# Constant tables gated on steps of the first attention, and a rewritten order of steps, in a fused attention and Fourier-mix kernel

## The chip, the cores and the metric

The kernel runs on one core of a Trainium2 chip. The time is the device time of one execution in microseconds (us). A core has a matmul engine (PE, with its weight loads, PEld), a vector engine (DVE), a scalar engine (ACT), a general engine (POOL, GpSimd) and a queue engine (SP). POOL and SP also issue DMAs.

## The reference, cut to what matters

The program is block attention with a learned soft permutation of blocks, then a Fourier mix with a two-layer MLP.

```python
# batch 4, heads 8, seq 768, head_dim 64, 8 blocks of 96; d_model 512, hidden 2048
for _ in range(5):                       # Sinkhorn on sort_net, 8x8 per head
    P = exp(P - max(P)); P /= sum(P, -1); P /= sum(P, -2)
k_sorted, v_sorted = P @ k_blocks, P @ v_blocks
attn = softmax(q_block @ k_sorted_block.T / 8);  x = attn @ v_sorted_block
u = x + real(fft(fft(x, axis=seq), axis=d_model))
out = u + relu(layernorm(u) @ w_ch1) @ w_ch2
```

All of the inputs have to come in once: K, Q and V (6.3 MB each) and two weights (4.2 MB each), as float32, cast to float16 on the way. The Fourier transforms are matmuls against constant tables.

## The kernel before

The work is cut into some 530 small steps, each a function named by one letter and digits. A long string fixes the order in which the steps are written.

```python
ORDER = ("B2 B0 k00AA B1 M00 M01 M02 M03 x000 e000 k01DA H M04 M05 Z0 "
         "s03 s00 s04 s05 x011 e011 L20 D b0 x010 s02 s01 v20A V v31A "
         ... )
for tok in ORDER.split():
    fns[tok[0]](*[...digits of tok...])
W = (32, 8, 8)             # PE, DVE, ACT
for e, w in zip((EN.PE, EN.DVE, EN.Activation), W):
    for n in range(w, len(runs[e])):
        dep(runs[e][n], runs[e][n - w])   # n runs after the one w places before it
```

A scheduler may move an instruction within the window W of its engine, but no further. After compiling, each engine runs its list in order. The steps that matter here (the first digit is the batch, A or D names the engine, ACT or DVE, that copies a matmul result out):

- L20, L21, V: POOL issues the loads of K and Q of batch 2 (two halves) and of V of batches 2 and 3.
- k, q: sort and transpose K and Q; x, e: scores and their exponentials; M, Z, s: sum of V and V minus its mean, written into the tile vcx; v, w: sort V, matmuls that read vcx; o: attention output.
- f, c, d, l, n: Fourier folding on DVE, sequence transform, width transform with LayerNorm statistics, LayerNorm factors on POOL, normalisation.
- h, y: the two MLP layers, 896 of the 2,400 matmuls.
- q21, q20, ...: for later batches Q is rearranged by DVE (copy qr<-q) and transposed by DMA:

```python
def t_q(b, hp, eng="S"):
    ...
    if eng == "S":
        qr = wt([128, 6, 2, D], F16, "qr", 1)
        nc.vector.tensor_copy(qr, q16.rearrange("p h r d -> p r h d"))
        nc.sync.dma_start_transpose(qt, qr.rearrange("p r h d -> p (r h d)"))
```

The tables are loaded right after the Sinkhorn iterations (ph is the list of their last DVE steps; gated(x, y) lets x wait for y, start(x) keeps x in program order). The first, dtab, lands in a part of the weight tile w2sb, and POOL copies it to unused columns of vcx.

```python
dst = w2sb.rearrange("p c m -> p (c m)")[:, 0:1024]
gated(nc.sync.dma_start(dst, cn["dtab"]...), ph[7])
start(nc.gpsimd.tensor_copy(vcx[:, 0:8, 96:128, :], dst...))
...  # then tab, cs, lt and small rows on the SP queue
for c in range(4):
    w = nc.gpsimd.dma_start(w1sb[:, c, :], w1v[:, c, :])
    gated(w, ph[9]) if c == 0 else start(w)
for c in range(4):
    start(nc.gpsimd.dma_start(w2sb[:, 4 * c:4 * c + 4, :], ...))
...
def t_v(n, bb, eng):      # sorts V: reads whole rows of vcx, also columns 96:128
    for dd in range(8):
        nc.tensor.matmul(ps[:, dd, :], vcx[:, 2 * n + dd // 4, :, dd % 4], bd)
```

The softmax here doesn't subtract the row's maximum and nothing guards it: scores larger than these inputs give would overflow.

## Time and profile before

| | before |
|---|---|
| time, median | 297.5 us (3 runs); 297.77, 298.32, 298.03 and 298.00 in the later sets |
| span of the profiled run | 296.2 us |
| PE busy | 274.7 us, 93% of the span |
| DVE, ACT, POOL busy | 64%, 41%, 13% |

The table of stretches gives, for each stretch of time, the busy time of PE, PEld, DVE, ACT and POOL with the number of instructions, then the granted PE clock (1.00 is full), the DMA share and GB/s. Lines for short stretches in which PE starves, and two long ones from later:

```profile
20.00:24.00 4.00, 2.57 (x43) 2.23 (x44) 4.00 (x9) 2.18 (x7) 0.05 (x1) 0.91 1.23 246
24.00:28.00 4.00, 3.61 (x62) 3.14 (x57) 3.79 (x12) 3.47 (x8) 1.02 (x2) 0.50 1.32 203
44.00:48.00 4.00, 1.43 (x39) 1.16 (x37) 3.86 (x10) 2.93 (x7) 1.08 (x2) 0.90 1.24 218
48.00:52.00 4.00, 4.00 (x33) 3.24 (x32) 3.50 (x9) 1.98 (x4) 0.75 (x1) 0.50 1.24 211
56.00:60.00 4.00, 1.28 (x19) 0.84 (x17) 1.72 (x4) 0.63 (x2) 0.00 (x0) 1.00 1.10 222
60.00:64.00 4.00, 3.56 (x36) 2.12 (x37) 3.23 (x9) 1.88 (x5) 0.00 (x0) 0.60 1.05 203
...
100.00:120.00 20.00, 20.00 (x189) 12.64 (x189) 12.80 (x29) 11.52 (x26) 0.76 (x2) 1.00 0.08 27
240.00:260.00 20.00, 20.00 (x114) 10.90 (x112) 11.76 (x23) 1.96 (x4) 0.00 (x0) 1.00 0.14 47
```

From about 64 us on PE is nearly always busy (its longest wait is then 0.4 us) and at full clock. Before that it starves three times (at about 22, 45 and 57 us), and each time the clock falls to one half for a while. The Trainium skill's page "TensorE: Matmul & The Clock Gate", Part 1, says that an idle window of about 3.4 us throttles the clock. The trace agrees in the lengths: its clock records show half clock at 23.3-30.1, 47.2-54.0 and 60.8-64.2 us, which is 6.8, 6.8 and 3.4 us. It does not show a whole idle window first: PE's longest waits there were 1.2, 1.6 and 2.7 us, and PE was busy for 2.4, 1.4 and 1.1 us of the 3.4 us before each fall.

The waits of PE in the list of waits (us in total, times, longest):

```profile
PE pf L276 <- DMA q<-in_q_dram: 8.6, 1, 8.6
PE pf L465 <- DVE u L661: 2.7, 1, 2.7
PE pf L626 <- DVE ee L597: 1.6, 1, 1.6
PE pf L448 <- DMA k<-in_k_dram: 1.2, 1, 1.2
```

The third starvation comes from DVE. Its timeline (start, duration, engine, line, operation, what it writes and reads; in brackets the idle time before it and what ended it):

```profile
54.66 0.25 DVE L641 TENSOR_SCALAR yr<-y 128x384 f16<-128x384 f16 x1
58.25 0.36 DVE L269 COPY qr<-q 128x768 f16<-128x768 f16 x1 [3.33 <-DMA q<-in_q_dram]
58.52 0.68 DVE L661 SCALAR_TENSOR_TENSOR u<-r,pf 128x512 f32<-128x512 f16 x1
```

DVE stood 3.33 us before the copy qr<-q, because Q of batch 2 had not landed. The step u behind it, which frees a buffer that PE needs, had its input from PE at about 55.1 us (the matmul L657 ran from 54.69 to 55.07). This stop of DVE before qr is called the gate below. POOL's timeline shows where that load stands in the queue:

```profile
17.32 1.04 POOL L309 COPY vcx<-w2sb 128x1024 f16<-128x1024 f16 x1 [4.10 <-DMA w2sb<-k_dtab]
18.30 1.08 POOL L328 DMA_DIRECT2D w1sb<-in_moe_w_ch_dram  x2
38.90 0.74 POOL L169 DMA_DIRECT2D q<-in_q_dram  x1 [1.45 <-DMA w1sb<-in_moe_w_ch_dram]
```

The issue at 38.90 us landed 19.3 us later, at 58.2. DMA moves about 215 GB/s in nearly every slice from 4 to 64 us, so each load lands when all that stands before it has been moved.

### The profile page before, as it was taken

Reading aid. Unit: us, or ns where it says so; the run is one execution under the profiler, and the core shown is the slowest. Engines: PE = TensorE matmul, PEld = TensorE weight load, DVE = VectorE, ACT = ScalarE, POOL = GpSimd, SP = SyncE. Lnnn points to the kernel's source line nnn. Section 1 sums busy time; section 2 is a strip of 40 time slices with the busy share of each in tenths; the row PEclk is TensorE's granted clock in tenths of the full one; section 3 lists DMA queues with packets and bytes.
Section 4 is the critical chain, followed back from the end, with each engine's and each line's share of the span. In section 5 each row is a group of like instructions: output and inputs, shape, how many; then the busy total and the mean of one; then the engine's idle time right before and its main releaser. Section 6 shows DMA issues by size and latency. Waiting matters only on the chain.

```text
span 296.2 us, 5916 instructions
## 1 busy us (share of the span) xinstructions
PE 274.7 (93%) x2395; PEld 165.9 (56%) x2395; DVE 190.0 (64%) x451; ACT 122.4 (41%) x260; POOL 39.3 (13%) x75
## 2 busy tenths in 40 slices
PE   0897986699999999999999999999999999999994
PEld 0366875456564666755565557546645555555551
DVE  6568699388887765666976578639716736643312
ACT  2358766348867755640477125203610111121210
POOL 8722332012020000400020002000200200020000
PEclk9995996879999999999999999999999999999999
DMA  7999999995179110481323101220031021033002
GB/s 113 219 300 205 214 209 215 214 180 76 22 43 124 39 38 35 53 123 38 110 58 62 55 35 38 54 73 35 19 38 71 37 55 71 35 37 124 1 2 106
DMA packets 32706, 26.48 MB, mean 89 GB/s; under 512 B 17347, under 2 KB 28099, under 8 KB 32676
## 3 DMA queue, kind: packets, MB, share of 16 engines
q0 software_dynamic: 11712, 13.63, 28.3%
q1 hardware_dynamic: 20966, 12.46, 17.1%
q8 instruction: 19, 0.31, 0.4%
q14 instruction: 9, 0.07, 0.1%
HBM read 29.10 MB, written 6.29 MB: 119 GB/s over the span
## 4 chain that ended last, share of the span: by engine, by line
PE 76%; DMA 13%; POOL 5%; DVE 2%; issue 2%; ACT 0%; POOLq 0%
PE pm L724 28%; PE pm L712 28%; DMA w1sb<-in_moe_w_ch_dram 7%; DMA q<-in_q_dram 7%; PE pf L497 4%; PE pf L653 3%; PE pf L626 3%; PE pf L465 2%; PE pf L448 2%; PE pf L657 2%; PE pm L435 2%; POOL kq L179 1%; PE pm L378 1%; POOL k L169 1%; POOL q L169 1%
## 5 line engine op out<-in xcount | busy, mean ns | idle before, releaser
L712 PE MATMUL pm<-ut,w1sb 128*128 128x384 f16 x512 | 94.3, 326 | 0.0
L724 PE MATMUL pm<-w2sb,hr 128*128 128x512 f16 x384 | 90.0, 379 | 0.0
L712 PEld LDWEIGHTS <-w1sb 128*128 128x128 f16 x512 | 47.6, 98 | 30.9 <-issue 0.5
L717 ACT ACTIVATE hr<-pm 128x384 f16<-128x384 f32 x69 | 33.8, 492 | 71.4 <-PE pm L712 71.2
L724 PEld LDWEIGHTS <-hr 128*128 128x128 f16 x384 | 36.5, 98 | 39.4
L715 DVE TENSOR_SCALAR hr<-pm 128x384 f16<-128x384 f32 x59 | 32.5, 554 | 20.4 <-PE pm L712 19.2
L728 DVE TENSOR_TENSOR u<-pm,u 128x512 f32<-128x512 f32 x24 | 16.2, 687 | 37.4 <-PE pm L724 37.4
L469 ACT ACTIVATE ex<-pf 96x384 f32<-96x384 f32 x64 | 28.2, 487 | 24.8 <-PE pf L465 20.3
L673 POOL TENSOR_SCALAR mv<-mv 128x3 f32<-128x3 f32 x8 | 2.0, 251 | 183.4 <-DVE mv L667 150.9
L497 PE MATMUL pf<-vsf,eb 97*128 97x96 f16 x384 | 23.4, 208 | 0.0
L481 DVE TENSOR_SCALAR eb<-ex 96x384 f16<-96x384 f32 x64 | 20.7, 349 | 3.2 <-ACT ex L469 3.0
L497 PEld LDWEIGHTS <-eb 97*128 97x128 f16 x384 | 19.9, 98 | 4.6 <-issue 0.3
L661 DVE SCALAR_TENSOR_TENSOR u<-r,pf 128x512 f32<-128x512 f16 x24 | 16.2, 681 | 5.8 <-PE pf L657 5.3
L256 ACT CAST vsf<-pm 96x512 f16<-96x512 f32 x24 | 16.5, 739 | 7.9 <-PE pm L435 7.2
L465 PE MATMUL pf<-qt,ksb 64*128 64x96 f16 x256 | 13.2, 205 | 4.8 <-DVE u L661 2.7
L506 DVE TENSOR_TENSOR r<-pf,rz 128x384 f16<-128x384 f32 x32 | 17.4, 548 | 0.4
L688 ACT ACTIVATE un<-u,nm,ny 128x512 f16<-128x512 f32 x16 | 12.8, 811 | 11.2 <-POOL nm L677 4.9
L666 DVE BATCH_NORM_STATS2 st<-u 128x6 f32<-128x512 f32 x24 | 16.3, 682 | 0.1
L465 PEld LDWEIGHTS <-ksb 64*128 64x128 f16 x256 | 7.9, 94 | 13.6 <-issue 10.0
L256 ACT CAST ksb<-pf 128x384 f16<-128x384 f32 x21 | 9.6, 480 | 4.8 <-PE pf L448 4.6
L276 PE MATMUL pf<-pack,q 128*64 128x128 f16 x48 | 3.5, 281 | 8.6 <-DMA q<-in_q_dram 8.6
L448 PE MATMUL pf<-bdk,k 128*64 128x128 f16 x144 | 8.7, 233 | 1.5 <-DMA k<-in_k_dram 1.2
(110 smaller groups left out, 296.3 us busy)
## 6 DMA issues: line engine op xcount, KB each, us to landing
out_dram<-u SPq DMA_DIRECT2D x24, 256.0 KB, 2.0
vst<-in_v_dram POOLq DMA_DIRECT2D x4, 768.0 KB, 16.5
k<-in_k_dram POOLq DMA_DIRECT2D x6, 384.0 KB, 13.9
q<-in_q_dram POOLq DMA_DIRECT2D x6, 384.0 KB, 14.2
w1sb<-in_moe_w_ch_dram POOLq DMA_DIRECT2D x4, 512.0 KB, 17.6
w2sb<-in_moe_w_ch_dram POOLq DMA_DIRECT2D x4, 512.0 KB, 19.5
kq<-in_k_dram POOLq DMA_DIRECT2D x2, 384.0 KB, 19.0
kq<-in_q_dram POOLq DMA_DIRECT2D x2, 384.0 KB, 20.2
```

Source lines behind the costliest of these rows:

```text
L256: nc.scalar.copy(dst, src)
L465: nc.tensor.matmul(pss[h2][:, j, :], ks[rows, 4 * g + j], qt[rows, :, cc])
L469: nc.scalar.activation(ex.rearrange("p j (c r) -> p j c r", r=6), pss[h2][0:96].rearrange("p j (r c) -> p j c r", c=16), AF.Exp, scale=SCALE)
L481: nc.vector.tensor_scalar(ed, exs[b, hp, g, h2], -1.0, None, op0=ALU.add)
L497: nc.tensor.matmul(po[:, 65 * T:65 * T + w], e[:, S * g + 256 * tt + 128 * n: S * g + 256 * tt + 128 * n + 128], vsf[:, vi:vi + w], start= ...
L506: nc.vector.tensor_tensor(rt[:, :, D * h:D * h + D], po3[:, :, 0:D], rz[:, :, None].broadcast_to([128, 6, D]), op=ALU.mult)
L661: nc.vector.scalar_tensor_tensor(u.rearrange("p (m n) -> p m n", n=2), rts[b][:, T, :].rearrange("p (m n) -> p m n", n=2), RSC, ps.rearran ...
L666: nc.vector.bn_stats(st, u)
L712: nc.tensor.matmul(ps, w1sb[:, c, 128 * fc:128 * fc + 128], uns[b, g][:, c, :], start=(c == 0), stop=(c == 3))
L715: nc.vector.tensor_scalar(hr[:, fc, :], ps, 0.0, None, op0=ALU.max)
L717: nc.scalar.activation(hr[:, fc, :], ps, AF.Relu)
L724: nc.tensor.matmul(ps, hrs[b, g][:, fc, 128 * tt:128 * tt + 128], w2sb[:, fc, :], start=(fc == 0), stop=(fc == 15))
```

## The change

The intent, as I read the diff: K and Q of the second half of batch 0 should not share the DMA with 1.64 MB of tables that are needed later. The tables, and with them the weight loads, now wait for DVE steps of the first attention. The order of all steps was written anew at the same time, and one idle matmul (step i) was left out. Cut to its core:

```diff
-    gated(nc.sync.dma_start(dst, cn["dtab"]...), ph[7])
-    start(nc.gpsimd.tensor_copy(vcx[:, 0:8, 96:128, :], dst...))
-    start(nc.sync.dma_start(tab, ...)); ... cs ...; ... lt ...
-    ... w1 and w2 loads ...
+    def t_C(n):
+        prev = [i for i in traced() if i.engine == EN.DVE][-1]
+        def late(w):
+            dep(w.ins, prev, mybir.DependencyClass.Sync)
+            start(w)
+        if n == 0:
+            late(nc.sync.dma_start(dst, cn["dtab"]...))
+            start(nc.gpsimd.tensor_copy(vcx[:, 0:8, 96:128, :], dst...))
+            ... w1 and w2 loads ...
+        elif n == 1: late(... tab)
+        elif n == 2: late(... cs)
+        else:        late(... lt) ...
-        "B2 B0 k00AA B1 M00 M01 M02 M03 x000 e000 k01DA H M04 M05 Z0 "
-        ... "c01 c02 c04 c03 r1 k11DA d00 e100 x110 q13D "
-        "q21 d01 e101 x111 o10 q12A d02 k12AA d03 d04 l00 ...
+        "B0 B1 H k00AD x000 C1 M00 k01AA x010 C0 C2 B2 M01 M02 M03 "
+        "M04 M05 e000 Z0 s02 s03 s04 D b1 x001 k02AA e001 L20 s05 s01 "
+        "x011 C3 e011 q02D x020 b0 s00 v60A v40A v10D v01D ...
+        ... "c00 q11D c01 r0 c02 c04 c03 k11AA x101 d00 d01 q13A "
+        "e100 q21 e101 x110 v71A d02 l00 x111 q12A o10 r1 k12AA ...
```

## The prediction

> **What bounds the kernel now.** In the table of stretches TensorE (PE) is busy 20.00 of every 20 us from 80 to 280 us at clock 1.00: from about 64 us on there is only matmul work, and the list of waits shows no PE wait after 76 us. So only what lies before it can be won. There PE idles 8.6 us until the first Q has landed, 2.45 us in 20-40 and 5.9 us in 40-60, and each gap is followed by a half-clock stretch (granted clock 0.50 in 24-28 and 48-52, 0.60 in 60-64), some 7 us of work lost by my estimate. This agrees with the Trainium skill's page "TensorE: Matmul & The Clock Gate", Part 1, where an idle window of about 3.4 us throttles the clock.
>
> DMA is saturated from 4 to 66 us: about 215 GB/s in every slice, share about 1.
>
> In the chain of waits, Q of batch 2 was issued at 38.9 us and landed at 58.2. VectorE (DVE), which runs in order, stood 3.33 us before its copy qr<-q, and PE waited 2.7 us for the DVE step behind it.
>
> **What the change does.** It removes no work but one idle matmul of 0.2 us. The constant tables dtab, tab, cs and lt (256+514+579+288 KB, 1.64 MB) were issued at 10.7-12.5 us and landed at 17-24 us, beside V and K/Q of the second half. Now they wait for DVE steps of the first attention, about 18-20 us. The skill's page "DMA: Bandwidth & Descriptors", Queues, rings and completion order, says that each engine takes turns between queues (here the 256 KB table took 6.6 us). At 215 GB/s 1.64 MB is 7.6 us of DMA time, so I expect K of that half at 17-19 us instead of 23.7 and Q at 19-21 instead of 26.2. PE's 1.2 us wait for k at 23.7 us goes, perhaps with the half-clock stretch behind it (3 us).
>
> But dtab now lands near 25 us, and the POOL copy out of it stands before w1 and w2. The w1 loads start near 26 us instead of 18.3. The four loads of batch 1 are still in flight then, so I expect no hole in the DMA stream. All bytes in front of batch 2's Q are the same as before, so it lands at 58 us again and takes back most of what was won before it. What stays: the new order puts the copy qr<-q behind two stages of d (per stage, DVE u 0.68 us and st 0.69 us), so 1 to 3 us more work is done when DVE is blocked.
>
> **Sum.** Up to 25 us: 2 to 4 us won; given back at the gate: 1 to 2; after it: about 1 won. Net about 2.5 us: **295.0 us**, range 291.5 to 298.0 (8 in 10). Faster by over 2% (under 291.5): 0.12; within 2%: 0.85; slower by over 2%: 0.03.
>
> **What would show it.** In the waits: PE<-DMA k gone; DVE qr<-DMA q still there near 58 us, as long as before or longer. In the table of stretches: granted clock in 24-28 above 0.5. w1 issued 6 to 9 us later, DMA share above 1 throughout 12-60.
>
> **What would make it wrong.** If the scheduler moved the qr copy elsewhere, or batch 2's Q lands earlier, the gate falls and 4 to 7 us are won. If dtab lands after 28 us, POOL starves the queue, everything lands later and the kernel is slower.

## The result, and the profile after

The changed kernel takes 295.8 us, median of 4 runs (295.03 to 295.97), against 297.77 for before (4 runs). The ratio is 0.9929, 95% interval 0.9906 to 0.9952. Ratios here are the mean time of one kernel's runs over the mean of the other's in the same rounds, so not quite the ratio of the medians quoted. The gain is about 2.1 us (0.0071 of 298), inside the range predicted and under 2%.

The same stretches after. The line numbers of the changed kernel are 11 higher after the table loads.

```profile
20.00:24.00 4.00, 3.76 (x54) 2.85 (x53) 3.41 (x7) 2.27 (x7) 0.00 (x0) 1.00 1.19 281
24.00:28.00 4.00, 1.06 (x24) 0.93 (x24) 4.00 (x10) 2.08 (x6) 1.78 (x1) 0.80 1.18 289
44.00:48.00 4.00, 3.04 (x56) 2.28 (x55) 4.00 (x13) 1.76 (x6) 0.84 (x1) 1.00 1.24 207
48.00:52.00 4.00, 1.78 (x22) 1.17 (x24) 3.86 (x8) 2.43 (x6) 0.75 (x1) 0.79 1.24 221
56.00:60.00 4.00, 3.97 (x61) 2.88 (x62) 3.09 (x10) 3.19 (x8) 0.00 (x0) 1.00 1.08 217
60.00:64.00 4.00, 3.94 (x50) 2.29 (x46) 3.41 (x10) 2.58 (x6) 0.86 (x2) 1.00 1.06 203
...
```

The starvation at 56-60 us and the half clock at 60-64 are gone. The other two are not: they come later, the first one deeper (PE 1.06 us busy in 24-28, where it was 3.61). The clock records show half clock at 26.4-33.2 and 50.3-53.7 us, 10.2 us in all instead of 17.1. PE's waits:

```profile
PE pf L276 <- DMA q<-in_q_dram: 8.4, 1, 8.4
PE pm L437 <- DVE vcx L424: 2.9, 1, 2.9
PE pf L476 <- ACT ksb L256: 1.5, 1, 1.5
PE pf L637 <- DVE ee L608: 0.9, 1, 0.9
```

PE's wait for K has gone, as have the 2.7 us for u. A new wait of 2.9 us stands before the V matmuls. DVE's timeline shows the steps in front of it, and then the copy qr:

```profile
24.89 0.35 DVE L492 TENSOR_SCALAR eb<-ex 96x384 f16<-96x384 f32 x1
25.16 1.21 DVE L374 TENSOR_TENSOR bdk<-tkh,pack 128x1024 f16<-128x1024 f16 x1
26.56 0.68 DVE L424 TENSOR_TENSOR vcx<-vst,vbn 128x1024 f16<-128x1024 f16 x1
...
57.21 0.69 DVE L672 SCALAR_TENSOR_TENSOR u<-r,pf 128x512 f32<-128x512 f16 x1 [0.91 <-PE pf L668]
57.81 0.35 DVE L269 COPY qr<-q 128x768 f16<-128x768 f16 x1
58.08 0.69 DVE L677 BATCH_NORM_STATS2 st<-u 128x6 f32<-128x512 f32 x1
```

The V matmuls wait for the last subtraction into vcx (26.56), which now stands behind an exponential step and the mask product of batch 1 (25.16), a step that is needed only much later. At the other end, DVE now comes to qr at 57.81 us and does not wait. POOL's timeline, and then the chain of waits (start, duration, what):

```profile
26.22 2.19 POOL L328 COPY vcx<-w2sb 128x1024 f16<-128x1024 f16 x1 [12.99 <-DMA w2sb<-k_dtab]
28.36 2.25 POOL L332 DMA_DIRECT2D w1sb<-in_moe_w_ch_dram  x4
38.02 0.74 POOL L169 DMA_DIRECT2D q<-in_q_dram  x1 [1.47 <-DMA w1sb<-in_moe_w_ch_dram]
```

```profile
18.12 8.04 DMA w2sb<-k_dtab
26.22 2.20 POOL vcx L328
28.46 0.62 PE pm L437 x8
```

K of the second half landed at 18.4 us (issue 4.01 plus 14.4) instead of 23.7, Q at 20.3 instead of 25.9. Q of batch 2 was issued at 38.0 and landed at 57.3. So the loads came as predicted. But dtab, now behind a DVE step of the attention, took 8.0 us. POOL's copy of it then took 2.2 us instead of 1.04, and the V matmuls at 28.46 us waited for that copy. They read whole rows of vcx, also the columns that the copy fills. In this run the copy itself cost PE little: the V matmuls that do not need it began at 27.39 us, after the subtraction, and the wait for the copy was 0.2 us. It lies just behind the DVE steps, though, and shows as soon as they are moved away (e1, e3). The Trainium skill's page "GPSIMD Engine Reference", Specifications, says that POOL shares its SBUF interfaces with DVE, with contention when a DVE instruction runs in a 2-port performance mode or has two SBUF inputs. The trace fits that: the end of the mask product (to 26.37) and the subtraction at 26.56, which have two SBUF inputs, run during the copy, and wherever no such step overlapped it (before, and e1, e3 and e7 below) the copy took 1.04 us. In all three profiles with a slow copy (2.19 us here and in e0, 2.26 us in e11) it ended 1.17 us after the end of that subtraction, hardly more than its own 1.04 us, as if it had waited for it. DVE was held up as well: exponential steps that began during the copy took 1.50 us for three in e1 (0.89 in before) and 1.23 us for two in e3 (0.61 in e7). That the overlap is the cause was not tested alone.

By the step ee, the Fourier folding of the first batch, the changed kernel is 2.8 us behind before. The first line is from before, the second from the changed kernel:

```profile
46.77 0.97 DVE L597 TENSOR_TENSOR ee<-pmt 128x1542 f16<-128x1542 f16 x1
49.54 0.97 DVE L608 TENSOR_TENSOR ee<-pmt 128x1542 f16<-128x1542 f16 x1
```

It ends about 2 us ahead. So the gain was made after that point.

### The profile page after: what moved, and what is told of

Read it like the earlier page. It is cut to its first block, busy times and chain, and to the rows that moved or that the text cites. A ratio compares the mean times of both kernels' runs of the same rounds, so it can differ in the third digit from the quotient of the medians.

```text
span 293.3 us, 5936 instructions
## 1 busy us (share of the span) xinstructions
PE 272.8 (93%) x2406; PEld 164.4 (56%) x2406; DVE 190.3 (65%) x450; ACT 122.3 (42%) x261; POOL 41.0 (14%) x75
## 4 chain that ended last, share of the span: by engine, by line
PE 82%; DMA 12%; POOL 2%; DVE 1%; ACT 1%; issue 1%; SPq 0%; POOLq 0%
PE pm L735 29%; PE pm L723 28%; DMA vst<-in_v_dram 7%; PE pf L508 5%; PE pf L664 3%; PE pf L637 3%; DMA w2sb<-k_dtab 3%; PE pf L476 2%; DMA q<-in_q_dram 2%; PE pf L459 2%; PE pm L437 2%; PE pm L247 2%; PE pf L668 2%; PE pm L446 1%; PE pf L276 1%; PE pm L389 1%
## 5 line engine op out<-in xcount | busy, mean ns | idle before, releaser
L723 PE MATMUL pm<-ut,w1sb 128*128 128x384 f16 x512 | 97.4, 326 | 0.0
L735 PE MATMUL pm<-w2sb,hr 128*128 128x512 f16 x384 | 94.7, 379 | 0.0
L728 ACT ACTIVATE hr<-pm 128x384 f16<-128x384 f32 x73 | 35.5, 489 | 77.9 <-PE pm L723 77.6
L726 DVE TENSOR_SCALAR hr<-pm 128x384 f16<-128x384 f32 x55 | 30.3, 553 | 25.8 <-PE pm L723 24.9
L492 DVE TENSOR_SCALAR eb<-ex 96x384 f16<-96x384 f32 x64 | 21.5, 352 | 6.2 <-ACT ex L480 4.8
L508 PE MATMUL pf<-vsf,eb 97*128 97x96 f16 x384 | 22.5, 207 | 0.8 <-DVE eb L492 0.8
L256 ACT CAST vsf<-pm 96x512 f16<-96x512 f32 x19 | 13.3, 736 | 11.8 <-PE pm L446 10.0
L677 DVE BATCH_NORM_STATS2 st<-u 128x6 f32<-128x512 f32 x24 | 16.2, 680 | 0.1
L699 ACT ACTIVATE un<-u,nm,ny 128x512 f16<-128x512 f32 x14 | 11.2, 812 | 8.9 <-DMA ut<-un 6.6
L258 DVE CAST vsf<-pm 96x512 f16<-96x512 f32 x13 | 9.6, 745 | 6.3 <-PE pm L446 3.5
L516 DVE RECIPROCAL rz<-pf 128x6 f32<-128x6 f32 x32 | 5.9, 186 | 9.4 <-PE pf L508 9.2
## 6 DMA issues: line engine op xcount, KB each, us to landing
vst<-in_v_dram POOLq DMA_DIRECT2D x4, 768.0 KB, 16.2
```

The source lines that it names most:

```text
L492: nc.vector.tensor_scalar(ed, exs[b, hp, g, h2], -1.0, None, op0=ALU.add)
L508: nc.tensor.matmul(po[:, 65 * T:65 * T + w], e[:, S * g + 256 * tt + 128 * n: S * g + 256 * tt + 128 * n + 128], vsf[:, vi:vi + w], start= ...
L677: nc.vector.bn_stats(st, u)
L723: nc.tensor.matmul(ps, w1sb[:, c, 128 * fc:128 * fc + 128], uns[b, g][:, c, :], start=(c == 0), stop=(c == 3))
L726: nc.vector.tensor_scalar(hr[:, fc, :], ps, 0.0, None, op0=ALU.max)
L728: nc.scalar.activation(hr[:, fc, :], ps, AF.Relu)
```

## The experiments

All were timed in five rounds beside the kernel before, four kernels on one chip at a time. The kernel before was at 298.32 us in the first set, 298.03 in the second and 298.00 in the third (11 runs each).

| run | median us | ratio to before | 95% interval |
|---|---|---|---|
| e1 tables late, old order | 297.16 | 0.9952 | 0.9924-0.9980 |
| e2 new order, tables early | 295.63 | 0.9913 | 0.9893-0.9934 |
| e3 changed, V steps first | 295.36 | 0.9909 | 0.9886-0.9931 |
| e6 before, qr copy later | 295.66 | 0.9920 | 0.9895-0.9946 |
| e0 changed, again | 296.09 | 0.9929 | 0.9905-0.9953 |
| e7 e3 with dtab early | 295.41 | 0.9907 | 0.9889-0.9926 |
| e8 e7 with Q and V before the weights | 294.75 | 0.9878 | 0.9851-0.9905 |
| e9 e8 with V sums in the hole | 294.99 | 0.9899 | 0.9868-0.9930 |
| e4 old head, new tail | 297.15 | 0.9969 | 0.9939-0.9998 |
| e10 old head with qr later, new tail, e8's loads | 291.31 | 0.9779 | 0.9754-0.9804 |
| e11 changed, more DVE work | 296.68 | 0.9957 | 0.9933-0.9981 |
| e12 e8 with less DVE work | 293.79 | 0.9862 | 0.9837-0.9886 |

My theory at the start was that the new order brings the gain, because it no longer stops DVE before qr. The rival was the stated intent: the early K and Q bring it.

### The two halves of the change, one at a time (e1, e2)

The compiled lists of PE, DVE and ACT of e1 are those of before, and those of e2 are those of the changed kernel. So within each pair only the DMAs and POOL differ.

```diff
 e1:  -"B2 B0 k00AA B1 M00 ..."             (tables early)
      +"B2 B0 k00AA B1 C1 C0 C2 M00 ..."    (t_C of the change; C3 after s01)
 e2:  ORDER of the changed kernel without C0 to C3; table and weight loads as in before
```

> The order of before, with only the tables (dtab, tab, cs, lt) and the w1/w2 loads moved behind steps of the first attention as in the changed kernel; the instruction order of PE, DVE and ACT is the same as in before, so only the DMA differs. Theory 'order' (the gain comes from where the written order puts the qr copy of batch 2 and from the dense part, and early K/Q of the second half is given back at batch 2's Q): 297.0 to 298.2 us, PE's 1.2 us wait for k gone, DVE still waiting 2.5 us or more before qr near 57 us. Rival 'tables' (the gain comes from K and Q of the second half landing 5 us earlier): 295.4 to 296.4 us.

> The changed kernel's order with the tables and w1/w2 loaded as in before; the engines' instruction order is that of the changed kernel, so only the DMA differs. Theory 'order': 295.4 to 296.6 us, most of the gain, with K of the second half again at about 23.7 us and PE waiting for it. Rival 'tables': 297.3 us or more, slower than before if the order was made for early K and Q.

The order alone gives all of the gain: 0.9913, against 0.9929 for both together. The tables alone give a part, 0.9952. The two do not add. On top of the new order the late tables show no gain at all; that they cost something (0.9929 against 0.9913) is within the intervals. This decides for the order. In e2 PE still waits 1.6 us for the DVE subtraction with the tables early, so that part of the new stall belongs to the order. Yet e1, at the lower end of what my theory had for it, is 1.4 us faster than before by its ratio: the late tables do carry something in the old order. Three lines of e1's list of waits show what was won and given back:

```profile
PE pm L437 <- POOL vcx L328: 3.3, 1, 3.3
DVE qr L269 <- DMA q<-in_q_dram: 2.4, 1, 2.4
PE pf L476 <- DVE u L672: 1.8, 1, 1.8
```

PE's wait for K is gone. In its place PE stands 3.3 us for POOL's copy of dtab, which shows the hidden dependence without the new order. DVE's stop before qr is 2.4 us instead of 3.3, because Q of batch 2 landed at 57.9 instead of 58.2 and DVE came to it later, and PE waits 1.8 us behind it instead of 2.7.

### The position of one copy (e6)

```diff
-"... k11DA d00 e100 x110 q13D q21 d01 e101 x111 o10 q12A d02 k12AA ..."
+"... k11DA d00 e100 x110 q13D d01 e101 x111 o10 q12A d02 q21 k12AA ..."
```

> Before, with only the step q21 (DVE copy qr and its transposing DMA) moved nine steps later, behind d02; tables early as in before. Theory 'gate': DVE no longer stands 3.3 us before qr, the half-clock stretch at 60.8 to 64.2 us goes, 295.2 to 296.4 us, that is most of the change's gain without moving a table. Rival 'tables': the wait comes back at V of batch 2 or in LayerNorm, 297.0 us or more.

One step was moved in the written order (in the compiled lists some neighbouring steps of DVE, ACT and PE changed places too), and the kernel is at 295.66 us, ratio 0.9920: as good as the changed kernel. DVE came to the copy at 59.75 us and went on:

```profile
54.95 0.69 DVE L661 SCALAR_TENSOR_TENSOR u<-r,pf 128x512 f32<-128x512 f16 x1 [0.19 <-PE pf L657]
59.66 0.17 DVE L667 BATCH_NORM_AGGREGATE mv<-st 128x2 f32<-128x6 f32 x1
59.75 0.32 DVE L269 COPY qr<-q 128x768 f16<-128x768 f16 x1
```

The step u runs at 54.95 us, 3.6 us earlier than in before. A new wait takes back a part of it. It is the first of these two lines from the list of waits:

```profile
PE pm L378 <- DMA vst<-in_v_dram: 2.7, 1, 2.7
PE pf L626 <- DVE ee L597: 1.6, 1, 1.6
```

PE now comes to the sums of V of batch 2 before that V has landed. So what followed the stop was again a load.

### Is the new stall before the V matmuls worth anything? (e3, e7)

```diff
 e3 (on the changed kernel):
-"... e001 L20 s05 s01 x011 C3 e011 q02D x020 b0 s00 v60A ... o03 T1 o02 q03A L21 ..."
+"... e001 L20 s05 s01 s00 b0 x011 C3 e011 q02D x020 v60A ... o03 o02 q03A T1 L21 ..."
 e7 (on e3): dtab's load and POOL copy early again, as in before; tab, cs, lt stay late
```

> The changed kernel with the last V subtraction (s00) ahead of two exp steps and the batch 1 mask product (T1) later, so that DVE's work no longer stands in the way of PE at 24.3 to 27.4 us. PE's wait of 2.9 us there should fall to about 1. Theory 'gate' (before 57 us nothing counts, since batch 2's Q lands then and DVE stands before qr): DVE waits 1 to 2 us before qr, total within 0.6 us of the changed kernel, 295.2 to 296.2. Rival (every stall removed before 60 us is won): 293.6 to 294.6 us.

> As run e3_v_first (engines' instruction order the same), but the small table dtab (256 KB) and its POOL copy early again as in before; only tab, cs and lt late. Theory 'hidden wait' (in the changed kernel the POOL copy of dtab writes into the vcx tile that the V matmuls read, so the late table holds them up): PE no longer waits for POOL's copy, the V matmuls start at about 25.5 us, 294.4 to 295.3 us, that is 0.3 to 0.8 us under e3_v_first. Rival (the copy is beside the critical path, and all before Q and V of batch 2 is swallowed): no difference to e3_v_first, within 0.3 us.

In e3 PE's wait of 2.9 us became 1.5 us for ACT and 1.1 us for POOL's copy. In e7 the wait for POOL is gone too: the V matmuls start at 26.51 us (27.39 in the changed kernel; in e3 the first 16 at 26.18 and the next only at 28.06). The times are 295.36 and 295.41 us, and the changed kernel beside e7 took 296.09. So the rival of e3 (all of it is won) fell, and so did my expectation for e7 of 0.3 to 0.8 us: the wait for the copy is real, but taking it away moved nothing that can be told from noise (the intervals are about 0.6 us to either side). The part of my gate theory that DVE would stand 1 to 2 us before qr again was wrong too: it did not wait there in either run. The traces show where the lead went. In e7 the DVE step that writes atp runs at 37.20 us (38.55 in the changed kernel) and ee at 48.92 (49.54), but the first u only at 57.41 (57.21). In between PE has half clock from 44.6 to 54.8 us in e7, and from 50.3 to 53.7 in the changed kernel. So the time won was lost beside a longer half-clock stretch, not at the gate; no run separates the two.

### Are the late loads of batch 2 the limit? (e8, e9)

```diff
 e8 (on e7):  "... L20 ... v70A V v11A ..." with C0 (now only the weight loads) after V
 e9 (on e8):
-"... f02 k10AA ... c00 q11D ... x120 M10 M11 d05 ... M12 ... M13 ... M14 M15 ..."
+"... f02 M10 M11 M12 k10AA ... c00 M13 M14 M15 q11D ... x120 d05 ..."
```

> As e7_dtab_early, but POOL issues K and Q of batch 2 and V of batches 2 and 3 ahead of the weights w1 and w2; engines' instruction order the same. Q of batch 2 should land at 33 to 40 us instead of 57 and that V at 42 to 52 instead of 61 to 65. Theory 'gate' (their landing limits what is won before 60 us): 293.0 to 294.3 us. Rival (in this order DVE and PE arrive at them too late for it to matter): within 0.3 us of e7_dtab_early.

> As e8_qv_before_weights, with the 12 matmuls of 0.22 us that sum V of batches 2 and 3 (M10 to M15) moved from about 61-68 us into PE's idle stretch at 47 to 51 us, before the Fourier step, which the early V allows. If that idle stretch and the half-clock stretch behind it are what is left to win: 290.5 to 292.5 us and half-clock time before 60 us under 10 us. If V lands after 48 us or DVE is the limit there: 293 us or more.

In e8 Q of batch 2 landed at 36.7 us (issue 20.5 plus 16.2) and all of V by about 44 us. The time is 294.75 us, 0.7 under e7, less than the theory had asked for; the intervals overlap. In e9 the holes before the Fourier step are filled (the wait for ee is gone from the list of waits), and nothing was won: 294.99 us. The stretches of e9 and its longest new wait show where it went:

```profile
48.00:60.00 12.00, 11.73 (x166) 8.15 (x164) 10.81 (x27) 8.51 (x20) 0.84 (x2) 0.99 1.16 213
60.00:72.00 12.00, 10.03 (x113) 7.24 (x110) 11.90 (x32) 8.66 (x19) 3.70 (x8) 0.72 0.94 146
```

```profile
PE pf L710 <- ACT un L699: 2.0, 1, 2.0
```

DVE is busy 11.90 of 12 us in 60-72. PE stands before the LayerNorm output, which waits for the DVE statistics, and the half clock has moved to 65.2-72.0 us. In e9's chain of waits there are only DVE steps from 56.35 to 62.71 us, then POOL's LayerNorm factors and ACT. So with the loads out of the way, DVE limits the stretch that ends at the first MLP layer in e9.

### More and less DVE work (e11, e12)

```diff
 e11 (on the changed kernel), in t_d, for b == 0 and the first three tiles:
+            st2 = wt([128, 6], F32, "st2", 1)
+            extra.append(nc.vector.bn_stats(st2, u).ins.name)   # kept out of the window W
 e12 (on e8): q11D -> q11A, n001DA -> n001AA
```

> The changed kernel with three statistics steps of DVE done twice (0.68 us each, 2.0 us in all, between about 58 and 64 us); results unused. Theory 'DVE' (between 57 and 75 us DVE is what limits: it has no slack left once qr no longer stops it): 1.2 to 2.2 us over the changed kernel, ratio to before 0.997 to 1.000. Rival 'PE' (matmul work is already what limits from 57 us on): within 0.5 us of the changed kernel, ratio 0.992 to 0.9945. A few neighbouring DVE and PE steps change places in the compiled order.

> As e8_qv_before_weights, with two copies moved from DVE to ACT (Q of batch 1, second pair, 0.55 us, and one LayerNorm step of batch 0, 0.51 us). Theory 'DVE': 0.4 to 1 us under e8_qv_before_weights, ratio to before 0.984 to 0.9865. Rival 'PE': no difference beyond 0.3 us.

In e11 the 2.0 us of DVE work cost about 0.8 us (ratio 0.9957 against 0.9929, from different sets). That is between the two theories, and the intervals overlap, so it does not decide. PE's wait for the LayerNorm output grew from 0.5 to 1.3 us in the profile, which fits a stretch that DVE limits in part. In e12 about 1.06 us less on DVE gave 0.9862 after 0.9878 (again from different sets), 0.5 us; the size fits theory "DVE", but the intervals overlap widely.

### Head and tail (e4), and the parts put together (e10)

The steps up to about 80 us are the head, the others, nearly all of them MLP, are the tail. e4 has the old head and the new tail. e10 has the head of e6, the new tail and the loads of e8.

> The order of before up to the seventh MLP tile of batch 0 (about 80 us), then the remaining steps in the order of the changed kernel; tables early as in before. The head's PE, DVE and ACT order is that of before, with its 3.3 us DVE stall. Theory 'stall' (all of the gain is in the head, before 80 us): 297.3 to 298.3 us, as before. Rival 'tail' (the new order of the dense part, with fewer changes between 64-row and 128-row matmuls, brings more than half of it, 1.6 us by my count of the profiled runs): 296.0 to 296.9 us.

> The head of before with the qr copy later (as e6_qr_later), K/Q of batch 2 and V ahead of the weights (as e8_qv_before_weights), tables tab, cs, lt late, and the tail in the changed kernel's order. If head and tail gains add: 293.3 to 294.6 us. If the tail brings nothing: 295.2 to 296 us.

e4, with its stop before qr still there (3.5 us), is at 0.9969, interval 0.9939 to 0.9998: the new tail is worth about 0.9 us, just clear of none; among twelve comparisons one so narrow can be chance. The changes between 64-row and 128-row matmuls that the expectation names do get fewer: from 80 us on the traces count 47 in before and 38 in e4. Whether they are the cause was not tested. e10 is at 291.31 us (5 runs, 291.00 to 292.04), ratio 0.9779: 2.2% under before, and about 4.5 us under the changed kernel by the two ratios, which come from different sets; its interval reaches 0.9804, so whether it is over 2% is not settled. Added up by ratios, the parts measured apart (e6 0.0080, the late tables 0.0048 as in e1, the tail 0.0031, the loads 0.0029 from e7 to e8) make 0.0188; e10 has 0.0221. With the errors of five ratios that is about their sum; that they bring more together is not shown. In e10's list of waits no wait of PE after the first Q is longer than 1.7 us, its chain of waits has only PE steps from 47.7 to 63.8 us, and its stretches show PE full where before starved:

```profile
48.00:60.00 12.00, 12.00 (x142) 8.88 (x141) 10.15 (x28) 7.72 (x16) 0.99 (x2) 0.79 1.16 211
60.00:72.00 12.00, 11.39 (x133) 7.26 (x131) 11.62 (x30) 9.19 (x20) 4.38 (x8) 1.00 0.93 146
```

The half clock has not become less: e10 has it at 22.2-29.0 and 42.7-52.9 us, 17.0 us in all, as much as before. A part of the 12.00 us busy in the first line is PE at half speed.

How much work is done early can be read from the group of the first MLP layer, listed for 80 us to the end: before, the changed kernel and e10 have 484, 476 and 464 of its 512 matmuls still to do. One line each:

```profile
L712 PE MATMUL pm<-ut,w1sb 128*128 128x384 f16 x484 | 89.0, 326 | 0.0
```

```profile
L723 PE MATMUL pm<-ut,w1sb 128*128 128x384 f16 x476 | 90.7, 326 | 0.0
```

```profile
L723 PE MATMUL pm<-ut,w1sb 128*128 128x384 f16 x464 | 88.4, 326 | 0.0
```

## Why the prediction was right or wrong

The total was right: 295.0 us predicted, 295.8 measured, in the range, and "within 2%" had 0.85. The sum behind it was right in part.

- **Right:** the loads. K of the second half came at 18.4 us (17-19 predicted), Q at 20.3 (19-21), dtab at 26.2 (near 25), Q of batch 2 at 57.3 (58). PE's wait for K went. The DMA share stayed above 1 from 12 to 60 us, so there was no hole in the stream. The weights were issued 10 us later (predicted 6 to 9; by the time given, 28.4 for 26).
- **Wrong: "Up to 25 us: 2 to 4 us won".** Nothing was won there. The first PE stall got longer, 2.9 us instead of 1.2, its half-clock stretch only moved from 23.3 to 26.4 us, and by the first Fourier folding the kernel was 2.8 us behind. I had counted what the DMA frees and not what stands before the V matmuls: DVE's order, and POOL's copy of dtab into the tile that they read. The copy was in the prediction as standing before the weights, not as an input of these matmuls. e1 shows it alone, 3.3 us of PE waiting. In e3 and e7, with both mended, the kernel gains 0.6 to 0.7 us by the ratios (0.9909 and 0.9907 against 0.9929), which is not clear of noise.
- **Wrong: "DVE qr<-DMA q still there near 58 us, as long as before or longer".** The wait was zero. Q landed when predicted, but DVE came to the copy at 57.8 us, because it was late and had u before it. So "given back at the gate: 1 to 2" did not happen either; the gate was where the gain came from. That rests on e2 (the order brings it) and e6 (the copy alone brings as much in the old order); no run put the copy back to its early place in the new order.
- **Right in mechanism, too small in size: "What stays: the new order puts the copy qr<-q behind two stages of d".** In fact the compiled order put it behind only the first u. This was the term I gave "about 1 won" net; e6 shows that moving this copy alone in the old kernel brings 2.4 us (0.0080 of 298).
- **Left out:** the tail, about 0.9 us by e4, an interval that barely excludes nothing.

So the terms were wrong in opposite directions and the errors cancelled: too much for the early loads, too little for the gate and the tail. That the total came out so close was luck.

What stays open: how far the stretch from 57 to 76 us is limited by DVE in the changed kernel (e11 paid 0.8 of 2.0 us), why late tables help in the old order by 1.4 us when only some 0.9 us of it is seen at the stop before qr, what decides how long each half-clock stretch lasts, and what in the new tail is faster.

## What to carry to other kernels

An engine that runs in order turns an early request for late data into a stop for everything behind it: look at what stands behind a DMA wait, and move the step that waits before you move any data. When a load is moved, follow every reader of the tile it ends in, also of its unused columns, and ask what else the matmuls behind it need. A stall taken away early may be worth nothing in the end (e3, e7), so follow the lead from step to step through the profile and see where it is lost. Parts that each bring under 1% can bring 2.2% together (e10), about their sum.

## What the Trainium skill lacked or had wrong

- "DMA: Bandwidth & Descriptors", Queues, rings and completion order, says that the engines take turns between queues packet by packet, but not what share of the bytes a queue then gets: a 256 KB table on the SP queue took 6.6 us and 8.0 us here beside the float32 to float16 loads of POOL.
- "TensorE: Matmul & The Clock Gate", Part 1, gives one idle window of about 3.4 us as what throttles the clock. The same part tells of a kernel in which many short idles between groups of matmuls made the clock go up and down. Here much less than an idle window was enough: before the three falls in the kernel before, no wait of PE was longer than 2.7 us, and in e7 PE was busy for 3.21 of the 3.40 us before the fall at 24.1 us. The lengths agree: the half-clock stretches were 3.4, 6.8 and 10.2 us long. The records of these runs show no other clock than 1.0 and 0.5.
